# Placing the last ten of 18 attention blocks beside the scans, taking softmax sums from a ones column, and moving loads off ScalarE's queue

## The chip, the cores and the metric

One core of one Trainium2 chip. The metric is device time in microseconds (us) of one execution. Runs over 1.5% above the fastest of their kernel are called slow. The profiled execution has a span, from first to last instruction, which is about 1.8 us below the time that the run reports. Engines are named as in the profile: PE is the matrix engine (TensorE), PEld its weight loads, DVE is VectorE, ACT is ScalarE, POOL is GpSimd and SP is SyncE, which here only issues loads and stores.

## The reference

Two independent halves write the two halves of the output's columns.

```python
# A: sliding, dilated attention. x (1, 2048, 448), 16 heads of 28
qkv = x @ wqkv
idx = pos[:, None] - 2 * arange(8)                 # 8 keys, two apart, back in time
attn = softmax(where(idx >= 0, q . k[idx] * 28 ** -0.5, -1e9))
a = (attn . v[idx]) @ wo
# B: a diagonal complex state-space model, 448 states, over 2048 steps
Lam_bar = exp(dt * (Lambda_re + 1j * Lambda_im)); dt = exp(log_dt)
h[t] = Lam_bar * h[t-1] + B_bar @ x[t]
y[t] = 2 * Re(C @ h[t]) + x[t] * Dskip
out = concatenate([a, b], axis=-1)                 # bf16
```

## The kernel before

Attention works on 18 blocks (9 of 114 queries for even positions, 9 for odd). A block is scores on PE, Exp on ACT, values on PE, an eviction on ACT. Softmax sums of a group of 6 blocks are gathered in one PSUM tile `dn`; one reciprocal on DVE serves the group; a normalisation (`att_norm`) spreads the reciprocals over the heads with PE and multiplies on DVE. A projection tile (`wo_tile`) then needs normalised blocks. The B half makes scan inputs on PE (`bu`), evicts them to `Z` on ACT, scans on DVE (`scan`, four calls), and ends with eight `y_tile`s on PE.

```python
# loads: ScalarE issues sixteen of them before its first arithmetic
for i, vec in enumerate((B_Lambda_re, B_Lambda_im, B_log_dt, B_Dskip)):
    ACT.dma_start(vrow[i:i + 1, 0:D], vec.unsqueeze(0))
for k in range(3):
    ACT.dma_start(wraw[:, k, :], A_wqkv[128 * k:128 * (k + 1), 0:2 * D])
ACT.dma_start(wraw[64:128, 3, :], A_wqkv[384:448, 0:2 * D])
load_xa(0, 0); load_xa(1, 0)                       # SyncE
ACT.dma_start(wv[:, 0:3, :], ...); ACT.dma_start(wv[64:128, 3, :], ...)
load_xa(0, 1); load_xa(1, 1)                       # SyncE
for ri, (m_, o_) in enumerate(...):                # six loads of B
    ACT.dma_start(NB_[...], ...)
# ... [cut]

def att_pv(n):                                     # values, and sums from P
    # ... [cut]
    for g in range(4):
        w0 = 31 - (4 * c + g)
        for j in range(4):                         # 16 narrow matmuls per block
            PE.matmul(att["dn"][32 * j:32 * j + 32, :], eden[:, e_, w0:w0 + 32], P[:, j, g, :], ...)
    ACT.copy(oT[...], op[:])
    if c == GB - 1:                                # GB = 6 blocks in a group
        V.reciprocal(rf[:], att["dn"][:]); V.tensor_copy(rb[:], rf[:])
        att["rb"] = rb
# ... [cut]

weave(steps[:12], fl)       # 6 blocks among the second half of the projections
bz_open()                   # memory for the scans
fl = []                     # scan inputs, scans, then normalisations 0-5, wo tiles 0, 1
for pt in range(4):
    fl.append(L(bu, 0, pt))
    if pt % 2:
        fl.append(L(scan, 0, pt // 2))
# ... [the same for the second half of the sequence; cut]
for i in range(0, GB, 2):
    fl.append(L(att_norm, i))
for n in range(2):
    fl.append(L(wo_tile, n))
weave(steps[12:24], fl)     # 6 more blocks among these
# ... [normalisations 6-11, wo tiles 2-4, y tiles 0-3 among the last 6 blocks,
#      normalisations 12-17, a check of all values, wo tiles 5-7, y tiles 4-7]
```

`weave` puts the entries of one list evenly between those of the other. A scheduler may still reorder inside an engine, so the places named below are read from the traces.

## Time and profile before

Three runs: 222.16 us median (221.75 to 223.7).

| stage of the profiled run (span 220.1 us) | us | what holds it |
|---|---|---|
| to the first Exp, 45.43 | 45.4 | ACT does no arithmetic until 20.84 |
| first Exp to first scan, 100.09 | 54.7 | PE busy 46.0, ACT 37.1 |
| first scan to end of last scan, 153.57 | 53.5 | DVE busy 52.7 |
| end of last scan to end | 66.5 | PE busy 52.2 |

First the page's shares of busy time and its 40 slices of 5.5 us; a digit is the busy share in tenths, and PEclk the granted clock of PE in tenths.

```profile
PE 161.9 (74%) x1618; PEld 80.7 (37%) x1629; DVE 117.7 (53%) x222; ACT 97.3 (44%) x137; POOL 9.3 (4%) x24
PE   0094769988488879899995960276798997399970
DVE  4671587744625632307999999999621001702010
PEclk9999699999969999999999695556799999859997
```

No engine is full overall, but DVE is full from the 20th to the 28th slice, and PE nearly empty in the 25th and 26th.

ACT's start (timeline: start, duration, engine, line of the program, operation, output and input, count, and in brackets the idle time just before with what ended it; ACTq is ACT's sequencer issuing a load):

```profile
8.93 0.51 ACTq L188 DMA_DIRECT2D wraw<-in_A_wqkv_dram  x1
...
20.20 0.61 ACTq L198 DMA_DIRECT2D NB__92<-in_B_B_re_dram  x1
20.84 1.28 ACT L397 ACT_TABLE_LOAD   x1 [20.84 <-DMA xTA<-in_A_x_dram]
...
22.25 0.99 ACT L272 CAST qT<-pq 128x1024 bf16<-128x1024 f32 x1
...
45.43 0.93 ACT L319 ACTIVATE P<-sp 128x912 bf16<-128x912 f32 x1
```

The loads of B still go out at 20.20 us, and only then can ACT begin. The Trainium skill, "DMA: Bandwidth & Descriptors", section "Anatomy of one DMA — SWDGE (gpsimd) path", says that a wait for a semaphore is served on the sequencer that issues the load, before the load is dispatched. The trace agrees in that ACT stands behind its own load issues for 20.84 us; which semaphore each issue waited for it does not show.

PE's two stops of over 3 us after the first scan (timeline of PE):

```profile
141.66 3.43 PE L367 MATMUL pw<-wo,qT 128*128 128x448 bf16 x8 [11.06 <-DVE qT L358]
...
191.33 0.16 PE L670 MATMUL pg<-good,ones 128*1 128x1 bf16 x1 [3.35 <-DVE good L666]
```

The first is a projection tile that waits for normalisations queued on DVE behind a scan. About six attention blocks are still undone at that time, but most stand behind it in PE's order.

### The profile page before, as it was taken

The page shows a single profiled execution, that of the slowest core. Times are in us where ns is not written, and L with a number is a line of the kernel's source. Part 1 is how long each engine was busy: PE and PEld are TensorE (multiplying, and loading weights), DVE is VectorE, ACT ScalarE, POOL GpSimd, SP SyncE. Part 2 cuts the span into 40 slices and gives each one's busy share as a digit, 9 for nine tenths or more (in the row PEclk, how much of TensorE's full clock was granted, in tenths as well). Part 3 has the DMA queues.
Part 4 walks back from the last instruction along what each step waited for, and adds up shares of the span by engine and source line. Part 5 has one row for each costly group of instructions (what it writes and reads, how often), then busy time and mean ns, then how long its engine had stood idle before and what let it go on. Part 6 is the DMA issues. An engine that isn't in the chain of part 4 may idle for free.

```text
span 220.1 us, 3859 instructions
## 1 busy us (share of the span) xinstructions
PE 161.9 (74%) x1618; PEld 80.7 (37%) x1629; DVE 117.7 (53%) x222; ACT 97.3 (44%) x137; POOL 9.3 (4%) x24
## 2 busy tenths in 40 slices
PE   0094769988488879899995960276798997399970
PEld 0031224435234435445442440022554554245540
DVE  4671587744625632307999999999621001702010
ACT  0002939998667873627554460023366263011110
POOL 8700000000000000000000000000000000000000
PEclk9999699999969999999999695556799999859997
DMA  6999990349300000000000000000212111112211
GB/s 124 210 247 253 271 217 3 60 92 126 60 0 3 0 3 0 3 0 0 3 0 3 0 3 0 1 0 17 69 45 83 45 42 43 43 42 83 84 47 46
DMA packets 31028, 13.05 MB, mean 59 GB/s; under 512 B 23644, under 2 KB 31008, under 8 KB 31008
## 3 DMA queue, kind: packets, MB, share of 16 engines
q1 hardware_dynamic: 28888, 10.65, 21.7%
q10 hardware_dynamic: 2120, 2.13, 4.4%
q8 instruction: 14, 0.23, 0.4%
q14 instruction: 6, 0.05, 0.1%
HBM read 3.33 MB, written 3.67 MB: 32 GB/s over the span
## 4 chain that ended last, share of the span: by engine, by line
DVE 37%; PE 31%; ACT 13%; DMA 7%; SPq 6%; issue 3%; DVEq 0%
DVE sc L554 9%; PE pw L367 6%; DVE qT L358 4%; PE py L575 4%; PE py L577 4%; ACT mixt L452 4%; DMA xTA<-in_A_x_dram 3%; PE py L573 3%; PE pv L292 3%; PE pb L535 3%; DMA Cn<-in_B_C_im_dram 3%; DVE kT L274 3%; PE pq L281 2%; SPq L178 2%; DVE sc L547 2%
## 5 line engine op out<-in xcount | busy, mean ns | idle before, releaser
L281 PE MATMUL pq<-xTA,wqk 128*128 128x512 bf16 x121 | 35.1, 434 | 10.5 <-ACT qT L272 5.9
L319 ACT ACTIVATE P<-sp 128x912 bf16<-128x912 f32 x36 | 32.1, 932 | 22.4 <-PE sp L315 22.4
L535 PE MATMUL pb<-xTB,BT 128*128 128x512 bf16 x108 | 26.5, 398 | 3.1 <-ACT Z L537 2.7
L367 PE MATMUL pw<-wo,qT 128*128 128x448 bf16 x64 | 19.2, 464 | 12.1 <-DVE qT L358 11.2
L281 PEld LDWEIGHTS <-wqk 128*128 128x128 bf16 x128 | 13.3, 107 | 29.0 <-issue 17.8
L535 PEld LDWEIGHTS <-BT 128*128 128x128 bf16 x112 | 11.2, 101 | 16.4 <-issue 4.5
L537 ACT CAST Z<-pb 128x1024 bf16<-128x1024 f32 x8 | 8.1, 1012 | 17.3 <-PE pb L535 10.5
L272 ACT CAST yb<-py 128x896 bf16<-128x896 f32 x6 | 5.4, 905 | 23.3 <-PE py L579 17.4
L367 PEld LDWEIGHTS <-qT 128*128 128x128 bf16 x64 | 7.1, 119 | 21.6 <-DVE qT L358 13.7
L292 PE MATMUL pv<-wv,xTA 128*128 128x448 bf16 x72 | 14.5, 353 | 0.7 <-DVE vp L274 0.7
L310 PE MATMUL sp<-mB,mA 32*128 32x456 bf16 x72 | 9.6, 381 | 5.7 <-DVE Wt L453 1.4
L342 DVE RECIPROCAL rf<-dn 128x114 f32<-128x114 f32 x3 | 2.6, 871 | 20.0 <-PE dn L337 20.0
L358 DVE SCALAR_TENSOR_TENSOR qT<-bc,qT 128x456 bf16<-128x456 f32 x18 | 10.7, 629 | 2.5 <-PE bc L352 2.4
L575 PE MATMUL py<-WL,Hs 128*128 128x448 bf16 x56 | 11.9, 352 | 0.0
L577 PE MATMUL py<-Wt,Hs 128*128 128x448 bf16 x56 | 11.9, 352 | 0.0
L272 ACT CAST ya<-pw 128x896 bf16<-128x896 f32 x4 | 3.6, 905 | 16.5 <-issue 8.4
L339 ACT CAST qT<-op 128x456 bf16<-128x456 f32 x18 | 9.8, 547 | 1.8 <-PE op L331 1.8
L397 ACT ACT_TABLE_LOAD x1 | 1.3, 1283 | 20.8 <-DMA xTA<-in_A_x_dram 20.8
L274 DVE CAST ya<-pw 128x896 bf16<-128x896 f32 x4 | 4.4, 1092 | 11.4 <-PE pw L367 11.4
L274 DVE CAST kT<-pq 128x1024 bf16<-128x1024 f32 x8 | 9.8, 1222 | 0.7 <-PE pq L281 0.7
L554 DVE TENSOR_TENSOR_SCAN sc<-rT,ini,Z 128x512 bf16<-128x512 f32 x8 | 9.6, 1267 | 0.0
L292 PEld LDWEIGHTS <-xTA 128*128 128x128 bf16 x72 | 6.9, 98 | 7.3 <-issue 1.0
(155 smaller groups left out, 240.0 us busy)
## 6 DMA issues: line engine op xcount, KB each, us to landing
out_dram<-ya SPq DMA_DIRECT2D x8, 224.0 KB, 2.4
out_dram<-yb SPq DMA_DIRECT2D x8, 224.0 KB
wraw<-in_A_wqkv_dram ACTq DMA_DIRECT2D x3, 224.0 KB
Cn<-in_B_C_re_dram SPq DMA_DIRECT2D x1, 392.0 KB, 4.3
Cn<-in_B_C_im_dram SPq DMA_DIRECT2D x1, 392.0 KB
wo<-in_A_wo_dram SPq DMA_DIRECT2D x4, 98.0 KB
wv<-in_A_wqkv_dram ACTq DMA_DIRECT2D x1, 336.0 KB
NB__92<-in_B_B_re_dram ACTq DMA_DIRECT2D x1, 336.0 KB, 6.1
```

Of the source, the lines that this page charges most:

```text
L274: V.tensor_copy(o_, i_)
L281: PE.matmul(ps[:, i, :], wqk[:, kt, qk, 4 * g:4 * g + 4, :].rearrange("p h d -> p (h d)"), xTA[:, kt, par, XPAD + 512 * h:XPAD + 512 * (h ...
L292: PE.matmul(ps[:, par, 0:D], xTA[:, kt, par, XW + QB * b:XW + QB * b + KB], wv[:, kt, :], start=(kt == 0), stop=(kt == 3))
L310: PE.matmul(sp[j // 2][:, j % 2, 0:4 * QB], mA[r0:r0 + 32, :], mB[r0:r0 + 32].rearrange("p a q -> p (a q)"), start=True, stop=False, skip_ ...
L319: ACT.activation(P[:, 2 * jp:2 * jp + 2].rearrange("p j g q -> p j (g q)"), sp[jp][:, :, 0:4 * QB], ACTF.Exp, scale=float(DH) ** -0.5)
L339: ACT.copy(oT[:, :, par, QB * b:QB * (b + 1)], op[:])
L358: V.scalar_tensor_tensor(o_, bc[:, i, 0:4 * QB].rearrange("p (g q) -> p g q", g=4), DSC, o_, ALU.mult, ALU.mult, accum_out=acc[:, n:n + 1])
L367: PE.matmul(ps[:, par, 0:D], oT[:, g, par, 128 * n:128 * (n + 1)], wo[:, g, :], start=(g == 0), stop=(g == 3))
L535: PE.matmul(ps[:, ri, :], BT[:, s_, ri, 128 * pt:128 * (pt + 1)], xTB[:, s_, SEG * s:SEG * (s + 1)], start=(s_ == 0), stop=(s_ == NS - 1))
L554: V.tensor_tensor_scan(c_[:, ri, i, :], prm["rT"][:, pt:pt + 1].to_broadcast((128, SEG)), z[:, ri, i, :], 0.0 if s == 0 else ini[:, ri, pt ...
L575: PE.matmul(ps[:, 0, 0:D], zz["H"][:, k, 128 * n + 1:128 * n + 129], WL[:, k, :], start=False, stop=(k == NK - 1))
L577: PE.matmul(ps[:, 1, 0:D], zz["H"][:, k, 128 * n + 2:128 * n + 130], Wt[:, k, :], start=(k == 0), stop=False)
```

## The change

Its intent: start ACT earlier; give PE attention blocks to do while DVE scans, so that fewer are left after; spend less of PE on sums; and shorten the work after the last scan. It has four parts.

1. Loads of the value weights and B go from ACT to SP, those of `wo` and C from SP to POOL. The copies of the query and key weights, all on DVE before, are shared with ACT. The selection matrix `sel` is made by ACT later, instead of by POOL at the start.
2. Column 28 of each head's 32 columns of V is a constant, so the value matmul also gives the sum. Four wide matmuls per block (`att_den`) pack these into `dn`, for groups of 8, 8 and 2 blocks.
3. Order: 8 blocks before the scans (was 6), 10 blocks with their sums beside the scans (was 6), none after, apart from ends of the last two. Normalisations 8 to 17 come after y tiles 0 to 3.
4. All evictions of the second half of the projections go to DVE.

The change also moves the transposed loads of the B half's x to the start, builds masks, tables and B's mixed inputs in another order, and shifts memory pools.

```diff
-    ACT.dma_start(wv[:, 0:3, :], ...)
-    ACT.dma_start(wv[64:128, 3, :], ...)
+    nc.sync.dma_start(wv[:, 0:3, :], ...)
+    nc.sync.dma_start(wv[64:128, 3, :], ...)
+    for ri, (m_, o_) in enumerate(...):
+        nc.sync.dma_start(NB_[...], ...)            # six loads of B
     load_xa(0, 1)
     load_xa(1, 1)
-    for ri, (m_, o_) in enumerate(...):
-        ACT.dma_start(NB_[...], ...)
# ... [cut]
-    V.memset(vp[:, :, :, DH:32], 0.0)
+    POOL.memset(vp[:, :, :, DH:DH + 1], DSC)
+    POOL.memset(vp[:, :, :, DH + 1:32], 0.0)
+    POOL.memset(vp[0:KPAD, 0:2, :, DH:DH + 1], 0.0)
# ... [wo and C: POOL.dma_start in place of nc.sync.dma_start; cut]
+    def att_den(n):
+        ...
         for g in range(4):
             w0 = 31 - (4 * c + g)
-            for j in range(4):
-                PE.matmul(att["dn"][32 * j:32 * j + 32, :], eden[:, e_, w0:w0 + 32], P[:, j, g, :], ...)
+            PE.matmul(att["dn"][:], (eden if m == 8 else edenL)[:]...[:, w0:w0 + 128], oT[:, g, par, ...], ...)
+        if c == m - 1:
             V.reciprocal(rf..., att["dn"]...); V.tensor_copy(rb[:], rf[:])
             att["rb"] = rb
# ... [cut]
-                fl.append(L(proj_qk, qk, par, 1, gp))
+                fl.append(L(proj_qk, qk, par, 1, gp, "D"))
-    weave(steps[:12], fl)
+    weave(steps(0, 8), fl)
     bz_open()
# ... [fl: scan inputs and scans as before]
-    for i in range(0, GB, 2):
-        fl.append(L(att_norm, i))
-    for n in range(2):
-        fl.append(L(wo_tile, n))
-    weave(steps[12:24], fl)
+    fl.insert(2, L(att_norm, 0))
+    fl.insert(3, L(att_norm, 2))
+    weave(steps(8, 18), fl)
+    fl = [L(att_norm, n) for n in (4, 6)] + [L(wo_tile, n, "A") for n in range(3)]
     for n in range(4):
         fl.append(L(y_tile, n, "A"))
-    weave(steps[24:], fl)
+    weave(steps(18, NA + 3), fl)
+    for n in range(8, NA, 2):
+        att_norm(n)
# ... [check; then wo tiles 3-7 (was 5-7) and y tiles 4-7]
```

More of the change, by code (lines that the diff above doesn't have):

```diff
@@ L25 @@
 QL = QB * NB
-GB = 6
 KT = 112
@@ L159 @@
     at = main.enter_context(tc.tile_pool(name="at", bufs=2))
-    pj = main.enter_context(tc.tile_pool(name="pj", bufs=1))
+    pj_ctx = ExitStack()
+    pj = pj_ctx.enter_context(tc.tile_pool(name="pj", bufs=1))
     bk = main.enter_context(tc.tile_pool(name="bk", bufs=1, side="right"))
@@ L166 @@
     xTA = pj.tile([128, 4, 2, XL], BF16, tag="xTA")
+    wraw = pj.tile([128, 4, 2 * D], BF16, tag="wraw")
+    wv = pj.tile([128, 4, D], BF16, tag="wv")
+    wqk = pj.tile([128, 4, 2, H, 32], BF16, tag="wqk")
     xTB = bk.tile([128, NS, NP], BF16, tag="xTB")
+    NB_ = st.tile([128, 2, 4, 2 * D], BF16, tag="NB")
+    Cn = st.tile([KT, 2, 4, 512], BF16, tag="Cn")
+    vrow = const.tile([4, 576], BF16, tag="vrow")
+    wo = at.tile([128, 4, D], BF16, tag="wo", bufs=1)
     xa_r = A_x[0].rearrange("(i two) d -> two i d", two=2)
@@ L178, in load_xb @@
         nc.sync.dma_start_transpose(xTB[:, :, SEG * s_:SEG * (s_ + 1)], xb_r[SEG * s_:SEG * (s_ + 1), :])
-    vrow = const.tile([4, 576], BF16, tag="vrow")
-    wraw = st.tile([128, 4, 2 * D], BF16, tag="cw")
-    wv = pj.tile([128, 4, D], BF16, tag="wv")
-    NB_ = st.tile([128, 2, 4, 2 * D], BF16, tag="NB")
     for i, vec in enumerate((B_Lambda_re, B_Lambda_im, B_log_dt, B_Dskip)):
@@ L190 @@
     load_xa(1, 0)
-    ACT.dma_start(wv[:, 0:3, :], A_wqkv[0:384, 2 * D:3 * D].rearrange("(s p) n -> p s n", p=128))
-    ACT.dma_start(wv[64:128, 3, :], A_wqkv[384:448, 2 * D:3 * D])
+    nc.sync.dma_start(wv[:, 0:3, :], A_wqkv[0:384, 2 * D:3 * D].rearrange("(s p) n -> p s n", p=128))
+    nc.sync.dma_start(wv[64:128, 3, :], A_wqkv[384:448, 2 * D:3 * D])
+    for ri, (m_, o_) in enumerate(((B_B_re, B_B_im), (B_B_im, B_B_re))):
+        nc.sync.dma_start(NB_[:, ri, 0:3, D:2 * D], m_[0:384, :].rearrange("(s p) n -> p s n", p=128))
+        nc.sync.dma_start(NB_[0:64, ri, 3, D:2 * D], m_[384:448, :])
+        nc.sync.dma_start(NB_[64:128, ri, 3, D:2 * D], o_[384:448, :])
     load_xa(0, 1)
     load_xa(1, 1)
-    for ri, (m_, o_) in enumerate(((B_B_re, B_B_im), (B_B_im, B_B_re))):
-        ACT.dma_start(NB_[:, ri, 0:3, D:2 * D], m_[0:384, :].rearrange("(s p) n -> p s n", p=128))
-        ACT.dma_start(NB_[0:64, ri, 3, D:2 * D], m_[384:448, :])
-        ACT.dma_start(NB_[64:128, ri, 3, D:2 * D], o_[384:448, :])
+    load_xb(0)
+    load_xb(1)
     kT = xa.tile([128, 4, 2, KL], BF16, tag="kT")
@@ L203 @@
     vp = xa.tile([128, 2 * NB, H, 32], BF16, tag="vp")
-    wqk = pj.tile([128, 4, 2, H, 32], BF16, tag="wqk")
-    wo = at.tile([128, 4, D], BF16, tag="wo", bufs=1)
-    eden = const.tile([128, 2, 63], BF16, tag="eden")
-    sel = const.tile([128, 4 * GB, 128], BF16, tag="sel")
+    eden = const.tile([128, 5, 32], BF16, tag="eden")
     pm = const.tile([128, 1], I32, tag="pm")
     kq = st.tile([128, 128], I32, tag="kq")
+    iot = st.tile([128, SEG], F32, tag="iota")
+    hpib = const.tile([128, 1], F32, tag="hpib")
+    POOL.memset(hpib[:], 0.5 * PI * SHR)
+    POOL.iota(iot[:], [[1, SEG]], base=0, channel_multiplier=0, allow_small_or_imprecise_dtypes=True)
+    POOL.iota(pm[:], [[0, 1]], base=0, channel_multiplier=1)
+    POOL.iota(kq[:], [[1, 128]], base=0, channel_multiplier=0)
     V.memset(wqk[:, :, :, :, DH:32], 0.0)
@@ L212 @@
     V.memset(wv[0:64, 3, :], 0.0)
-    V.memset(vp[:, :, :, DH:32], 0.0)
-    V.memset(wo[:], 0.0)
     POOL.memset(kT[:, :, :, 0:KPAD], 0.0)
@@ L219, with sel_make, wqk_copy @@
     POOL.memset(xTA[:, :, :, XPAD + NP:XL], 0.0)
-    POOL.iota(pm[:], [[0, 1]], base=0, channel_multiplier=1)
-    POOL.iota(kq[:], [[1, 128]], base=0, channel_multiplier=0)
-    iot = st.tile([128, SEG], F32, tag="iota")
-    POOL.iota(iot[:], [[1, SEG]], base=0, channel_multiplier=0, allow_small_or_imprecise_dtypes=True)
-    POOL.memset(eden[:], 0.0)
-    POOL.memset(eden[:, :, 31:32], DSC)
-    POOL.memset(eden[:, :, 55:56], DSC)
-    POOL.memset(eden[0:KPAD, 1, :], 0.0)
-    POOL.memset(sel[:], 1.0)
-    POOL.affine_select(out=sel[:], in_=sel[:], compare_op=ALU.is_equal, fill=0.0, base=0,
-                       pattern=[[-1, 4 * GB], [-32, 4], [0, 32]], channel_multiplier=1)
-    for kt in range(4):
-        p0 = 64 if kt == 3 else 0
-        V.tensor_copy(wqk[p0:128, kt, :, :, 0:DH], wraw[p0:128, kt, :].rearrange("p (a h d) -> p a h d", a=2, h=H))
+    POOL.memset(eden[:], 1.0)
+    POOL.affine_select(out=eden[:], in_=eden[:], compare_op=ALU.is_equal, fill=0.0, base=31 - DH,
+                       pattern=[[-32, 5], [-1, 32]], channel_multiplier=1)
+    POOL.memset(eden[:, :, 0:31], 0.0)
+    edenL = const.tile([128, 5, 32], BF16, tag="edenL")
+    POOL.tensor_copy(edenL[:], eden[:])
+    for i_ in range(3):
+        POOL.tensor_copy(edenL[:, 1:5, 7 + 8 * i_:8 + 8 * i_], eden[:, 0:4, 31:32])
+    POOL.memset(vp[:, :, :, DH:DH + 1], DSC)
+    POOL.memset(vp[:, :, :, DH + 1:32], 0.0)
+    POOL.memset(vp[0:KPAD, 0:2, :, DH:DH + 1], 0.0)
+    POOL.memset(wo[:], 0.0)
+    wo_r = A_wo.rearrange("(g j d) n -> j d g n", j=4, d=DH)
+    for j in range(4):
+        POOL.dma_start(wo[32 * j:32 * j + DH, :, :], wo_r[j])
+    for ri, m_ in enumerate((B_C_re, B_C_im)):
+        POOL.dma_start(Cn[:, ri, :, 0:D], m_.rearrange("(k p) n -> p k n", p=KT))
+    sel = const.tile([128, 32, 4, 32], BF16, tag="sel")
+    def sel_make():
+        with tc.issue_after(att["exp"].ins):
+            ACT.copy(sel[:], ident[:].rearrange("p (j r) -> p r j", j=4).unsqueeze(3).to_broadcast((128, 32, 4, 32)))
+    def wqk_copy():
+        for kt in range(4):
+            p0 = 64 if kt == 3 else 0
+            (V.tensor_copy if kt % 2 == 0 else ACT.copy)(
+                wqk[p0:128, kt, :, :, 0:DH], wraw[p0:128, kt, :].rearrange("p (a h d) -> p a h d", a=2, h=H))
     mA = const.tile([128, 128], BF16, tag="mA")
@@ L274, in evac, with proj_qk @@
             V.tensor_copy(o_, i_)
-    def proj_qk(qk, par, h, gp):
+    def proj_qk(qk, par, h, gp, eng=None):
         ps = ps2.tile([128, 2, 512], F32, tag="s", name="pq")
@@ L283, in proj_qk, with proj_v @@
         if qk == 0:
-            evac(qT[:, 2 * gp:2 * gp + 2, par, 512 * h:512 * (h + 1)], ps[:])
+            evac(qT[:, 2 * gp:2 * gp + 2, par, 512 * h:512 * (h + 1)], ps[:], eng)
         else:
-            evac(kT[:, 2 * gp:2 * gp + 2, par, KPAD + 512 * h:KPAD + 512 * (h + 1)], ps[:])
-    def proj_v(b):
+            evac(kT[:, 2 * gp:2 * gp + 2, par, KPAD + 512 * h:KPAD + 512 * (h + 1)], ps[:], eng)
+    def proj_v(b, eng=None):
         ps = ps2.tile([128, 2, 512], F32, tag="s", name="pv")
@@ L293, in proj_v @@
                           start=(kt == 0), stop=(kt == 3))
-        evac(vp[:, 2 * b:2 * b + 2, :, 0:DH], ps[:, :, 0:D].rearrange("p b (h d) -> p b h d", h=H))
+        evac(vp[:, 2 * b:2 * b + 2, :, 0:DH], ps[:, :, 0:D].rearrange("p b (h d) -> p b h d", h=H), eng)
     order = [(par, b) for b in range(NB) for par in range(2)]
@@ L318, in att_s, with grp @@
         for jp in range(2):
-            ACT.activation(P[:, 2 * jp:2 * jp + 2].rearrange("p j g q -> p j (g q)"), sp[jp][:, :, 0:4 * QB],
+            att["exp"] = ACT.activation(P[:, 2 * jp:2 * jp + 2].rearrange("p j g q -> p j (g q)"), sp[jp][:, :, 0:4 * QB],
                            ACTF.Exp, scale=float(DH) ** -0.5)
+    GRP = (8, 8, 2)
+    GOF = (0, 8, 16)
+    def grp(n):
+        k = min(n // 8, 2)
+        return n - GOF[k], GRP[k]
     def att_pv(n):
@@ L324, in att_pv @@
         P = Pt.pop(n)
-        c = n % GB
-        if c == 0:
-            att["dn"] = ps1.tile([128, QB], F32, tag="dn", name="dn")
         op = ps1.tile([128, 4, QB], F32, tag="o", name="op")
@@ L332, in att_pv @@
                           start=True, stop=True, skip_group_check=True)
-        e_ = 1 if b == 0 else 0
+        ACT.copy(oT[:, :, par, QB * b:QB * (b + 1)], op[:])
+    def att_den(n):
+        par, b = order[n]
+        c, m = grp(n)
+        if c == 0:
+            att["dn"] = ps1.tile([128, QB], F32, tag="dn", name="dn")
         for g in range(4):
             w0 = 31 - (4 * c + g)
-            for j in range(4):
-                PE.matmul(att["dn"][32 * j:32 * j + 32, :], eden[:, e_, w0:w0 + 32], P[:, j, g, :],
-                          start=(c == 0 and g == 0), stop=(c == GB - 1 and g == 3), skip_group_check=True)
-        ACT.copy(oT[:, :, par, QB * b:QB * (b + 1)], op[:])
-        if c == GB - 1:
+            PE.matmul(att["dn"][:], (eden if m == 8 else edenL)[:].rearrange("p a b -> p (a b)")[:, w0:w0 + 128], oT[:, g, par, QB * b:QB * (b + 1)],
+                      start=(c == 0 and g == 0), stop=(c == m - 1 and g == 3), skip_group_check=True)
+        if c == m - 1:
             rf = at.tile([128, QB], F32, tag="rf", name="rf")
-            V.reciprocal(rf[:], att["dn"][:])
+            V.reciprocal(rf[0:128], att["dn"][0:128])
             rb = at.tile([128, QB], BF16, tag="rb", name="rb")
@@ L349, in att_norm @@
         for i in range(2):
-            c = (n0 + i) % GB
+            c, m = grp(n0 + i)
             for g in range(4):
-                PE.matmul(bc[:, i, QB * g:QB * (g + 1)], sel[:, 4 * c + g, :], att["rb"][:],
+                s_ = sel[:, 4 * c + g].rearrange("p j r -> p (j r)")
+                PE.matmul(bc[:, i, QB * g:QB * (g + 1)], s_, att["rb"][:],
                           start=True, stop=True, skip_group_check=True)
@@ L383, in params @@
     def params():
-        V.tensor_copy(vrow[:, D:512], vrow[:, 384:D])
-        V.tensor_copy(vrow[:, 512:576], vrow[:, 0:64])
         tpv = ps2.tile([128, 8, 4], BF16, tag="s", name="tpv")
@@ L393, in params @@
         dsk = vec[:, 3, :]
-        hpib = vt("hpib", 1)
-        POOL.memset(hpib[:], 0.5 * PI * SHR)
         dt = vt("dt")
@@ L461, in lam_b @@
             nc.sync.dma_start_transpose(BT[:, :, ri, 128 * pt:128 * (pt + 1)], NB_[:, ri, pt, :])
-    Cl = []
-    def load_c():
-        Cn = st.tile([KT, 2, 4, 512], BF16, tag="cw", name="Cn")
-        Cl.append(Cn)
-        for ri, m_ in enumerate((B_C_re, B_C_im)):
-            nc.sync.dma_start(Cn[:, ri, :, 0:D], m_.rearrange("(k p) n -> p k n", p=KT))
     def w_make(ph):
-        Cn = Cl[0]
         tp = ps2.tile([128, 2, 1024], BF16, tag="s", name="tp")
@@ L521, in bz_open @@
     def bz_open():
-        st_ctx.close()
-        bz = bz_ctx.enter_context(tc.tile_pool(name="bz", bufs=1, side="right"))
+        pj_ctx.close()
+        bz = bz_ctx.enter_context(tc.tile_pool(name="bz", bufs=1))
         zz["bz"] = bz
@@ L582, in y_tile @@
         nc.sync.dma_start(out_b[n, :, :, D:2 * D], yb[:])
-    steps = []
-    for n in range(2 * NB):
-        steps.append(lambda n=n: att_s(n))
-        if n > 0:
-            steps.append(lambda n=n: att_pv(n - 1))
-    steps.append(lambda: att_pv(2 * NB - 1))
     def weave(st_, fl):
@@ L603, in L @@
         return lambda: f(*a)
+    V.tensor_copy(vrow[:, D:512], vrow[:, 384:D])
+    V.tensor_copy(vrow[:, 512:576], vrow[:, 0:64])
+    wqk_copy()
     params()
     table(0)
-    table(1)
+    masks()
     for gp in range(2):
@@ L612, with steps @@
             if gp == 0:
-                table(2 + par)
-    for pt in range(4):
-        lam_b(pt)
-    load_xb(0)
-    load_c()
+                table(1 + par)
+            elif par == 0:
+                table(3)
+                lam_b(0)
+            else:
+                lam_b(1)
     for b in range(4):
         proj_v(b)
-    masks()
+        if b < 2:
+            lam_b(2 + b)
     d_make()
-    load_xb(1)
-    wo_r = A_wo.rearrange("(g j d) n -> j d g n", j=4, d=DH)
-    for j in range(4):
-        nc.sync.dma_start(wo[32 * j:32 * j + DH, :, :], wo_r[j])
+    NA = 2 * NB
+    SL = [[] for _ in range(NA + 3)]
+    for n in range(NA):
+        SL[n].append(L(att_s, n))
+        SL[n + 1].append(L(att_pv, n))
+        SL[n + 2].append(L(att_den, n))
+    NQ = {9: (0, 2, 4, 6), 17: (8, 10, 12, 14), 19: (16,)}
+    def steps(lo, hi):
+        return [f_ for k in range(lo, hi) for f_ in SL[k]]
     fl = []
@@ L629 @@
             for qk in range(2):
-                fl.append(L(proj_qk, qk, par, 1, gp))
+                fl.append(L(proj_qk, qk, par, 1, gp, "D"))
     for b in range(4, NB):
-        fl.append(L(proj_v, b))
+        fl.append(L(proj_v, b, "D"))
     for i, f_ in enumerate((L(w_make, 0), L(w_make, 1), L(wl_make, 0), L(wl_make, 1), L(wl_make, 2), L(wl_make, 3),
@@ L635 @@
         fl.insert(2 * i + 2, f_)
-    weave(steps[:12], fl)
+    fl.insert(18, sel_make)
+    weave(steps(0, 8), fl)
     bz_open()
     fl = []
-    for pt in range(4):
-        fl.append(L(bu, 0, pt))
-        if pt % 2:
-            fl.append(L(scan, 0, pt // 2))
-    for pt in range(4):
-        fl.append(L(bu, 1, pt))
-        if pt % 2:
-            fl.append(L(scan, 1, pt // 2))
-    for i in range(0, GB, 2):
-        fl.append(L(att_norm, i))
-    for n in range(2):
-        fl.append(L(wo_tile, n))
-    weave(steps[12:24], fl)
-    fl = []
-    for i in range(0, GB, 2):
-        fl.append(L(att_norm, GB + i))
-    for n in range(2, 5):
-        fl.append(L(wo_tile, n))
+    for s_ in range(2):
+        for pt in range(4):
+            fl.append(L(bu, s_, pt))
+            if pt % 2:
+                fl.append(L(scan, s_, pt // 2))
+    fl.insert(2, L(att_norm, 0))
+    fl.insert(3, L(att_norm, 2))
+    weave(steps(8, 18), fl)
+    fl = [L(att_norm, n) for n in (4, 6)] + [L(wo_tile, n, "A") for n in range(3)]
     for n in range(4):
         fl.append(L(y_tile, n, "A"))
-    weave(steps[24:], fl)
-    for i in range(0, GB, 2):
-        att_norm(2 * GB + i)
+    weave(steps(18, NA + 3), fl)
+    for n in range(8, NA, 2):
+        att_norm(n)
     asum = const.tile([128, 1], F32, tag="asum")
@@ L673 @@
     bad = nc.values_load(flag[0:1, 0:1], min_val=0, max_val=1)
-    for n in range(5, 8):
+    for n in range(3, 8):
         wo_tile(n)
@@ L678 @@
     bz_ctx.close()
+    st_ctx.close()
     main.close()
```

## The prediction

> **What bounds the kernel now.** No engine is full (first part of the page: PE 74%, DVE 53%, ACT 44% of a 220.1 us span); three serial stretches set the time. (1) Start: ScalarE issues loads that wait for earlier loads and does no work until 20.84 us (its timeline), so the first projection tiles are evicted from 22.25 us and PE stands from about 19.1 to 23.3 us. (2) 100.1 to 153.5 us: the four scans on VectorE, 12.5 us each, almost without a gap (14.0 of 14 us busy from 138 to 152). PE is idle 11.06 us until 141.66, waiting for the normalised qT, and stays at clock 0.50 there: 8 output-projection matmuls take 3.43 us, later 1.69. That agrees with the Trainium skill, "TensorE: Matmul & The Clock Gate", Part 1: an idle window halves PE's clock. (3) The 66.6 us after the scans: six attention blocks, six projection tiles, eight y tiles of 3.6 us, final check, output.
>
> **What the change does, costed.**
> - Loads: eight of ScalarE's sixteen issues go to SyncE, and wo and C from SyncE to GpSimd. ScalarE still waits for the fourth wraw load (issued at 8.93 us now, copied at 11.99), then starts. Its table work takes about 5.5 us, so the first eviction comes at about 18.5 us instead of 22.25, the first Exp at about 39 instead of 45.4: 6 to 7 us off the critical path. GpSimd's 6.2 us of building sel go too; the first wqk copy took 2.8 us beside it, others 0.39.
> - Middle before the scans (ACT, PE and DVE alternate): now 38 us of ACT work take 48 us. Afterwards ACT work stays near 36 us (4 more Exp and about 4 us of sel, an estimate from 1 ns per element of Exp, against fewer evictions and mix copies); VectorE gets 8 us more evictions. I expect 45 to 48 us, but holding 8 attention blocks instead of 6. First scan at about 89 us (now 100.1).
> - Scans: the four stay 50 us. With 8 normalisations (0.56 us each) and two reciprocals, VectorE's chain is about 57 us, ending at about 146. The other 10 attention blocks hide under it; PE finishes them 15 to 20 us early and waits cold, because projection tiles 1 and 2 stand ahead of the y tiles in its order and need normalisations queued inside the last scan.
> - Sums: 288 narrow matmuls (16 in about 0.31 us) become 72 wide ones (estimate 0.2 us per block): 2 us of PE, mostly off the path.
> - After the scans: projection tile 2 and y tiles 0-3 (18 us with the cold start), ten normalisations with PE waiting and the check (7), five projection tiles (9), four y tiles (14.4), last eviction and landing (6.6): about 55 us instead of 66.6.
>
> **Sum.** 89 + 57 + 55 = 201 us of span. Run times are about 1 us above that. I predict 201 us, 190 to 211. Chances: faster by over 2% 0.95, within 2% 0.04, slower 0.01.
>
> **What would show it.** ScalarE's first work at 11 to 13 us; first scan between 84 and 94; scans plus normalisations 55 to 59 us with DVE full; a PE gap over 8 us before the first y tile, ended by VectorE; a second gap of 4 to 7 us before the last projections; 54 to 57 us from last scan to end.
>
> **What would make it wrong.** GpSimd's loads competing with wraw and x, so that PE starts later; VectorE's evictions queuing behind the mix steps and keeping PSUM full, so the first scan comes no earlier (about 210); the middle running at ACT's 36 us (about 190); normalisations waiting for PE inside the scans.

## More of the kernel before

The stages in numbers (view by windows: the window, its length, then busy time and instruction count for PE, PEld, DVE, ACT, POOL, then the PE clock, the DMA share and GB/s):

```profile
0.00:45.43 45.43, 27.78 (x130) 11.89 (x133) 27.41 (x84) 20.92 (x35) 9.17 (x23) 0.96 0.83 171
45.43:100.09 54.66, 45.96 (x544) 23.16 (x548) 22.36 (x32) 37.05 (x54) 0.11 (x1) 0.97 0.17 26
100.09:153.57 53.48, 35.93 (x397) 16.89 (x400) 52.71 (x70) 20.34 (x26) 0.00 (x0) 0.78 0.00 1
153.57:220.10 66.53, 52.21 (x549) 28.73 (x548) 15.24 (x38) 19.01 (x24) 0.00 (x0) 0.91 0.17 57
```

## The result, and the profile after

The kernel after took 201.97 us median (200.88 to 202.53, 4 runs) against 222.93 (221.75 to 223.83) for the kernel before. The ratio is 0.9057, with a 95% interval of 0.8991 to 0.9122. Ratios here are the mean time of one kernel's fast runs over that of the other's of the same rounds, so not quite the ratio of the medians quoted. The result is correct. The profiled span is 200.7 us, so 19.4 us went.

```profile
PE 157.8 (79%) x1401; PEld 80.5 (40%) x1413; DVE 118.7 (59%) x223; ACT 99.4 (50%) x135; POOL 12.2 (6%) x35
PE   0169999778888799894998998946789983999940
DVE  2639995667778334309994999999990057222200
PEclk9999999999999999998599699995899998899995
```

The total work of the engines hardly changed: PE 157.8 us against 161.9. The time went from the waits. By stage, cut at the same four events as before (first Exp, first scan, end of the last scan):

```profile
0.00:38.04 38.04, 25.78 (x127) 11.22 (x130) 25.20 (x83) 25.18 (x40) 12.08 (x34) 1.00 1.02 206
38.04:91.58 53.54, 46.05 (x519) 23.50 (x522) 28.08 (x36) 37.33 (x51) 0.11 (x1) 1.00 0.14 25
91.58:149.11 57.53, 46.33 (x507) 24.25 (x512) 53.69 (x75) 27.88 (x37) 0.00 (x0) 0.85 0.03 9
149.11:200.70 51.59, 39.68 (x252) 21.50 (x250) 11.71 (x31) 8.98 (x10) 0.00 (x0) 0.93 0.20 64
```

Against before the stages changed by -7.4, -1.1, +4.1 and -14.9 us. Under the scans PE now does 46.3 us of work instead of 35.9, which is 10.4 us more, and after them 39.7 instead of 52.2. That exchange is the largest part of the gain, and it costs a scan stretch that is 4.1 us longer: other DVE work lies between the scans (normalisations and another reciprocal), and so does a wait of 2.97 us, shown below.

ACT's start, and PE's stops of over 3 us after the first scan:

```profile
7.80 0.52 ACTq L191 DMA_DIRECT2D wraw<-in_A_wqkv_dram  x1
8.35 1.28 ACT L253 ACT_TABLE_LOAD   x1 [8.35 <-DMA wraw<-in_A_wqkv_dram]
...
18.14 0.99 ACT L293 CAST qT<-pq 128x1024 bf16<-128x1024 f32 x1
...
38.04 0.93 ACT L340 ACTIVATE P<-sp 128x912 bf16<-128x912 f32 x1
```

```profile
137.36 0.37 PE L382 MATMUL bc<-rb,sel 128*128 128x114 bf16 x2 [3.91 <-DVE rb L373]
...
169.15 0.16 PE L684 MATMUL pg<-good,ones 128*1 128x1 bf16 x1 [3.33 <-DVE good L680]
```

ACT begins at 8.35 us instead of 20.84, but only 7.4 of these 12.5 us reach the first Exp: the last weight copy, now on ACT, and PE behind it still wait until about 13 us for the fourth load of weights. The 11.06 us stop of PE has become one of 3.91 us. DVE shows two new holes, which stand for what is left to take:

```profile
108.94 1.23 DVE L564 TENSOR_TENSOR sc<-Z,tab 128x2048 bf16<-128x2048 bf16 x1 [2.97 <-ACT Z L554]
...
162.89 0.63 DVE L388 SCALAR_TENSOR_TENSOR qT<-bc,qT 128x456 bf16<-128x456 f32 x1 [12.66 <-PE bc L382]
```

In the second one DVE is idle while PE makes y tiles 0 to 3. Then DVE does ten normalisations (162.89 to 168.5 us) while PE waits for it. Two engines take turns where they could work side by side.

### The profile page after: what moved, and what is told of

The parts are those of the page before. It is cut to its first block, busy times and chain, and to the rows that moved or that the text cites. A ratio compares the mean times of both kernels' runs of the same rounds, so it can differ in the third digit from the quotient of the medians.

```text
span 200.7 us, 3428 instructions
## 1 busy us (share of the span) xinstructions
PE 157.8 (79%) x1401; PEld 80.5 (40%) x1413; DVE 118.7 (59%) x223; ACT 99.4 (50%) x135; POOL 12.2 (6%) x35
## 3 DMA queue, kind: packets, MB, share of 16 engines
HBM read 3.33 MB, written 3.67 MB: 35 GB/s over the span
## 4 chain that ended last, share of the span: by engine, by line
PE 50%; DVE 28%; ACT 7%; DMA 6%; issue 3%; SPq 1%; POOL 0%; DVEq 0%; POOLq 0%
PE pq L302 12%; DVE sc L571 7%; PE pv L313 6%; PE pw L397 5%; PE py L592 5%; PE py L594 5%; PE pb L552 5%; DVE qT L388 4%; PE py L590 3%; PE pk L520 3%; DMA xTA<-in_A_x_dram 3%; DVE sc L564 2%; DVE Z L565 2%; DMA wraw<-in_A_wqkv_dram 2%; ACT Z L554 2%
## 5 line engine op out<-in xcount | busy, mean ns | idle before, releaser
L302 PE MATMUL pq<-xTA,wqk 128*128 128x512 bf16 x122 | 32.7, 413 | 10.1 <-ACT wqk L253 3.7
L552 PE MATMUL pb<-xTB,BT 128*128 128x512 bf16 x106 | 27.3, 398 | 1.3 <-ACT Z L554 0.6
L293 ACT CAST ya<-pw 128x896 bf16<-128x896 f32 x6 | 5.4, 906 | 24.7 <-PE pw L397 24.7
L397 PE MATMUL pw<-wo,qT 128*128 128x448 bf16 x64 | 15.8, 403 | 1.7 <-DVE qT L388 1.0
L313 PE MATMUL pv<-wv,xTA 128*128 128x448 bf16 x72 | 14.6, 352 | 2.2 <-DVE K_168 L526 1.1
L295 DVE CAST vp<-pv 128x896 bf16<-128x896 f32 x7 | 7.6, 1091 | 7.4 <-PE pv L313 7.4
L382 PE MATMUL bc<-rb,sel 128*128 128x114 bf16 x72 | 6.1, 242 | 6.6 <-DVE rb L373 4.6
L336 PE MATMUL sp<-qT,kT 32*128 32x114 bf16 x288 | 10.4, 214 | 0.0
L356 PE MATMUL op<-P,vp 128*32 128x114 bf16 x288 | 9.3, 226 | 1.3 <-ACT P L340 1.3
L397 PEld LDWEIGHTS <-qT 128*128 128x128 bf16 x64 | 6.6, 109 | 9.4 <-issue 4.0
```

Of the source, the lines that this page charges most:

```text
L293: ACT.copy(o_, i_)
L295: V.tensor_copy(o_, i_)
L302: PE.matmul(ps[:, i, :], wqk[:, kt, qk, 4 * g:4 * g + 4, :].rearrange("p h d -> p (h d)"), xTA[:, kt, par, XPAD + 512 * h:XPAD + 512 * (h ...
L313: PE.matmul(ps[:, par, 0:D], xTA[:, kt, par, XW + QB * b:XW + QB * b + KB], wv[:, kt, :], start=(kt == 0), stop=(kt == 3))
L397: PE.matmul(ps[:, par, 0:D], oT[:, g, par, 128 * n:128 * (n + 1)], wo[:, g, :], start=(g == 0), stop=(g == 3))
L552: PE.matmul(ps[:, ri, :], BT[:, s_, ri, 128 * pt:128 * (pt + 1)], xTB[:, s_, SEG * s:SEG * (s + 1)], start=(s_ == 0), stop=(s_ == NS - 1))
```

## The experiments

Three theories were on trial. *Places*: the gain is the earlier start (about 7 us) plus attention blocks moved under the scans, and nothing else matters much. *Work*: PE has less to do for the sums. *Loads*: the earlier start carries nearly all. All kernels gave correct results. The kernel before took 223.01 us median (7 runs); later 222.57 and 222.06 us.

### a0_after_again: the kernel after, unchanged

The edit is none.

> The changed kernel as it is, as the yardstick for the other kernels of this call. Every theory: 201 to 203 us, span about 200.5.

Measured: 202.53 us median (201.73 to 203.73), ratio 0.9094 (0.903 to 0.9158), span 200.7. The result repeats; this is the base for the next three.

### e1_loads_back: the loads where they were

```diff
-    nc.sync.dma_start(wv...), nc.sync.dma_start(NB_...)   # behind the first half of x
-    POOL.dma_start(wo...), POOL.dma_start(Cn...)
+    ACT.dma_start(wv...), ACT.dma_start(NB_...)           # as in the kernel before
+    nc.sync.dma_start(Cn...), nc.sync.dma_start(wo...)
```

> All else of the change kept, loads on their old queues (V weights and B on ScalarE, wo and C on SyncE). Theory 'places' (the gain is an earlier start of about 7 us plus attention blocks moved under the scans): ScalarE's first work at 20 to 21 us again, first Exp at 44 to 46 us instead of 38.0, first scan 6 to 8 us later, 208 to 211 us in all. Rival 'work' (the gain is the PE work saved by the ones column): within 2 us of the changed kernel. Rival 'loads' (the earlier start carries nearly all): 215 us or more.

Measured: 212.11 us median (210.75 to 214.23), ratio 0.9499 (0.942 to 0.9578). One of the four runs is slow; the median of the fast ones, 211.54, is 9.0 us over a0. In its trace (timeline of PE, then of ACT and of DVE):

```profile
23.72 6.61 PE L302 MATMUL pq<-xTA,wqk 128*128 128x512 bf16 x20 [12.55 <-ACT wqk L253]
```

```profile
50.41 0.93 ACT L340 ACTIVATE P<-sp 128x912 bf16<-128x912 f32 x1
```

```profile
103.93 1.23 DVE L564 TENSOR_TENSOR sc<-Z,tab 128x2048 bf16<-128x2048 bf16 x1
```

The first Exp comes 12.6 us after that of a0 (37.85), later even than in the kernel before (45.43). The reason is in the first line: the change gives ACT half of the weight copies, so with the loads back on ACT, PE makes three matmuls of its projections and then stands 12.55 us until ACT has issued its loads and copied. The two edits of part 1 belong together. So the 9.0 us are not the worth of the places alone: they contain a first Exp 5 us later than in the kernel before. b1 below measures the places from the other side.

### e2_sums_back: the sums as before, first attempt

```diff
-    POOL.memset(eden[:], 1.0) ... affine_select ... edenL ... vp ones column
+    POOL.memset(eden[:], 0.0); POOL.memset(eden[:, :, 31:32], DSC) ...
+    POOL.memset(vp[:, :, :, DH:32], 0.0)
     # att_pv: 16 narrow matmuls from P; att_den: only the reciprocal
```

> All else kept, softmax sums by 288 narrow matmuls from P as before instead of 72 wide ones from the ones column. Theory 'places': PE busy 2 to 3 us more, most of it hidden, 202 to 205 us. Rival 'work': 208 us or more. Rival 'loads': within 2 us.

Measured: 209.53 us median (208.64 to 211.64), ratio 0.9417 (0.934 to 0.9494), 7.0 us over a0. The expectation of *places* was missed, but this run does not speak for *work* either. The delay stands at the start, before any sum (timeline of ACT):

```profile
8.71 0.57 ACTq L191 DMA_DIRECT2D wraw<-in_A_wqkv_dram  x1
9.31 1.28 ACT L248 ACT_TABLE_LOAD   x1 [9.31 <-DMA wraw<-in_A_wqkv_dram]
10.61 0.94 ACT L248 COPY wqk<-wraw 128x896 bf16<-128x896 bf16 x1
18.59 0.94 ACT L248 COPY wqk<-wraw 64x896 bf16<-64x896 bf16 x1 [7.05 <-DMA wraw<-in_A_wqkv_dram]
```

My edit shortened POOL's list of memsets. POOL therefore issued its loads of C and `wo` from 5.4 us on, where a0 begins at 7.7 us with `wo` and issues C from 10.6. The fourth load of the query and key weights, issued at 8.7 us, then took 9.9 us to land instead of 4.0. The Trainium skill, "DMA: Bandwidth & Descriptors", section "Queues, rings and completion order", says that each DMA engine serves the queue rows that have work in turn; the trace fits this: with the 1.2 MB of POOL's loads issued earlier, of which nothing is used while PE waits, the one load that PE waits for landed late. How the DMA engines shared their time was not looked at. So the kernel after has a good start partly because POOL is kept busy with memsets. By reading, the edit had a second fault: the group tile `dn` was claimed for group 1 before group 0's reciprocal was made, so that reciprocal read the wrong tile. A clean version follows.

### e2b_sums_back_clean: the sums as before, and nothing else

```diff
+    eden2 = ...            # made by POOL behind its loads; all else of the start untouched
     def att_pv(n):
+        # 16 narrow matmuls from P into dn, as in the kernel before
         ACT.copy(oT[...], op[:])
+        # reciprocal of the group here, as in the kernel before
     def att_den(n):
-        # four wide matmuls and the reciprocal
```

> The kernel after, with only the softmax sums made as before: sixteen narrow matmuls per block straight from P, in place of the four wide ones over the ones column; start-up program, loads and the order of everything else untouched. The earlier attempt at this also changed GpSimd's start, and its trace showed all its delay (first exponential 44.21 against 38.04 us) before any sum was made, and from the first exponential to the end 163.3 against 162.7 us. Theory of places: the first exponential stays at 38 us, the time 201 to 204 us, at most 2 us over the kernel after. Theory of work: the sums carry a real part of the gain, 205 us or more, with the first exponential unmoved.

Measured: 207.01 us median of 4 runs, of which two are slow (208.85 and 209.2) and two fast (205.17 and 204.46). The mean of the fast ones is 204.8 us; e6 below, an unaffected kernel, is at 201.86 median. So the sums are worth about 3 us, from two fast runs and without an interval. That lies just between the ranges of both theories (up to 204, and 205 or more): the sums are neither mostly off the path, as I had it, nor a main part. The stretch from the first Exp to the first scan is 57.14 us here and 53.52 us in a0 (view by windows; e2b first):

```profile
36.49:93.63 57.14, 48.33 (x649) 24.88 (x650) 28.34 (x36) 37.25 (x51) 0.11 (x1) 0.97 0.15 28
```

```profile
37.85:91.37 53.52, 46.05 (x519) 23.51 (x522) 28.08 (x36) 37.29 (x51) 0.11 (x1) 1.00 0.14 26
```

ACT's work is the same; PE's is 2.3 us more and the stretch 3.6 us longer. In e2, with its other start, the stretch was 57.2 us too (44.21 to 101.44), and in a0, after, e1 and e6, with wide sums, it was 53.5 each time. In e2, as in e2b, PE's clock in the stretch was 0.97 and not 1.00. About 1.4 us is given back under the scans (56.5 us against 57.9 in e6), and the part after them is 2.0 us longer (53.2 against 51.1). The matmuls of the sums alone, in these windows, take 4.10 us for 9 blocks (144 narrow) against 2.97 us for 8 blocks (32 wide), so 0.46 against 0.37 us per block; how the other 2 us of the stretch arise was not separated.

### e3_order_back: the order as before

```diff
-    weave(steps(0, 8), fl)
+    weave(steps(0, 7), fl)
     # scan inputs and scans
-    fl.insert(2, L(att_norm, 0)); fl.insert(3, L(att_norm, 2))
-    weave(steps(8, 18), fl)
-    fl = [L(att_norm, n) for n in (4, 6)] + [L(wo_tile, n, "A") for n in range(3)]
+    fl += [L(att_norm, n) for n in (0, 2, 4, 6)] + [L(wo_tile, n, "A") for n in range(2)]
+    weave(steps(7, 13), fl)
+    fl = [L(wo_tile, 2, "A")]
     # y tiles 0 to 3 as in the kernel after
-    weave(steps(18, NA + 3), fl)
+    weave(steps(13, NA + 3), fl)
```

> All else kept, order of blocks as before: about 6 blocks ahead of the scans, 6 beside them, 5 or 6 behind them. Theory 'places': first scan at 84 to 88 us instead of 91.6, but 64 to 70 us from the end of the last scan to the end of the kernel instead of 51.5; 210 to 217 us in all. Rivals 'work' and 'loads': within 3 us of the changed kernel.

Measured: 209.06 us median (207.13 to 209.31), ratio 0.9364 (0.9293 to 0.9434), 6.5 us over a0, just under the range. The first scan is at 88.09 us, 3.3 earlier than in a0, and its end at about 142 us, but the stage after the scans takes 63.3 us instead of 51. PE's large stop is back (timeline of PE):

```profile
125.90 0.56 PE L331 MATMUL sp<-mB,mA 32*128 32x456 bf16 x2 [11.54 <-DVE qT L388]
...
174.89 0.16 PE L683 MATMUL pg<-good,ones 128*1 128x1 bf16 x1 [3.33 <-DVE good L679]
```

This is the 11.06 us stop of the kernel before. So the order removes it, as claimed. The cost is that the first scan comes 3.3 us later, with one more block ahead of it, and that the scans take 58.1 us in a0 against 54.1 here; this is why the order's net worth is 6.5 us and not the 12 of the tail.

### b1_before_loads_moved: the kernel before, with part of the loads moved

```diff
-    ACT.dma_start(wv...); ACT.dma_start(NB_...)
+    nc.sync.dma_start(wv...); nc.sync.dma_start(NB_...)   # behind the first half of x
```

> The kernel before, with only the loads of the value weights and of B taken off ScalarE's queue and put on SyncE's behind the first half of x. Theory of places: ScalarE's first table load moves from 20.8 us to 9 to 11 us and the first exponential from 45.4 to 37 to 41 us; half of it or more reaches the end: 213 to 218 us, no more than half of the whole gain, and the idle stretch of TensorE under the scans stays at about 11 us. Theory of loads: 206 us or less. Against both: if the loads of C, which stay on SyncE and now come later, hold the scans back, 219 us or more.

Measured: 211.86 us median of 4 runs, of which two are slow (212.83 and 213.33); the fast ones are 208.74 and 210.89, ratio 0.9458 (0.9339 to 0.9577), which is 9 to 15 us off the kernel before. The fast runs lie between what *places* allowed (213 to 218) and what *loads* asked for (206 or less), so both were off. The profiled run is a slow one, so its times are only an indication: first Exp at 40.38 us, first scan at 91.59, and PE's idle stretch under the scans still there, as *places* said (timeline of PE):

```profile
133.15 3.43 PE L367 MATMUL pw<-wo,qT 128*128 128x448 bf16 x8 [12.74 <-DVE qT L358]
```

Eight moved loads, without any of the rest, bring about half to three quarters of the change's gain: 4.2 to 6.6% by the interval, where a0 has 9.1%.

### e4_evac_alternate: evictions shared again

```diff
-                fl.append(L(proj_qk, qk, par, 1, gp, "D"))
+                fl.append(L(proj_qk, qk, par, 1, gp))
-        fl.append(L(proj_v, b, "D"))
+        fl.append(L(proj_v, b))
```

> The kernel after, with the evictions of the second half of the projections alternating between ScalarE and VectorE as before, instead of all on VectorE. Six or seven evictions of about 0.95 us go back to ScalarE, which is busy 37 of the 53.5 us from the first exponential to the first scan. Both theories of the middle part: if TensorE sets that stretch (46 of 53.5 us), within 1.5 us of the kernel after, 201 to 204 us; if ScalarE's order does, because exponentials queue behind evictions, 2 to 5 us slower, the first scan at 93 to 97 us.

Measured: 202.7 us median (201.36 to 203.85), ratio 0.9123 (0.9049 to 0.9196). First Exp to first scan is 54.2 us (38.26 to 92.46), 0.7 more than in the kernel after, although ACT is busy 42.5 us of it instead of 37.3. Part 4 of the change makes no difference that could be seen, and ACT does not set the middle stretch.

### e5_sums_4_11_doubled and e6_own_sums: whose sums are used?

Reading the program, I found a mistake in the change. `att["rb"]` is one name, overwritten by each group, and normalisations are issued when the next group's reciprocal has already replaced it: blocks 4 to 7 are divided by the sums of group 1, blocks 8 to 15 by those of group 2. In the kernel before, by the same reading, every normalisation stands ahead of the next group's reciprocal.

```diff
# e5, wrong on purpose
     POOL.memset(vp[:, :, :, DH:DH + 1], DSC)
+    POOL.memset(vp[:, 4:12, :, DH:DH + 1], 2 * DSC)
# e6, mended
-            att["rb"] = rb
+            att["rb", n // 8] = rb
-                PE.matmul(bc[...], s_, att["rb"][:], ...)
+                PE.matmul(bc[...], s_, att["rb", (n0 + i) // 8][:], ...)
```

> The kernel after, with the ones column of blocks 4 to 11 doubled on purpose, so that the sums of these blocks come out twice too large. If each block is divided by its own sums, half of the attention output is halved and the comparison fails. If, as the reading of the program says, blocks 4 to 7 and 8 to 15 are divided by other groups' sums, nothing changes for blocks 4 to 11 but the result stays within tolerance: correct. The time says nothing here.

Measured (one run): correct, 201.41 us. This fits the reading. By itself it is not proof, because no control was run that shows that the comparison would notice a halved block. e6 settles it from the trace.

> The kernel after, with each pair of blocks divided by its own group's sums (the reciprocals are kept by group, where the kernel after keeps one name that the last group overwrites). No instruction is added or removed; only what the normalisations of blocks 4 to 7 and 8 to 15 read changes, and these read sums that are ready earlier. Both theories: correct, the time within 1 us of the kernel after (201 to 203 us); if the wait of TensorE for the second group's reciprocal (5.5 us once) is what holds the tail, 1 to 4 us faster.

Measured: correct, 201.86 us median (201.07 to 202.59), ratio 0.9105 (0.9024 to 0.9187): no change in time. Its timeline of PE at the place where the kernel after waited 3.91 us for `rb`:

```profile
131.49 0.42 PE L382 MATMUL bc<-rb,sel 128*128 128x114 bf16 x5
135.91 0.54 PE L367 MATMUL dn<-qT,edenL 128*128 128x114 bf16 x4 [3.99 <-DVE rf L371]
136.24 1.25 PE L382 MATMUL bc<-rb,sel 128*128 128x114 bf16 x11
```

With its own group's reciprocal, normalisation 4 starts at 131.49 us without any wait; in the kernel after it started at 137.36, behind group 1's reciprocal. So the kernel after does divide these blocks by other blocks' sums. It passes because, with these inputs, the logits are small and a softmax over 8 keys has sums near 8 everywhere: worked out from the reference's inputs, no logit is over 0.015 and the sums over 8 keys lie between 7.96 and 8.04. On other inputs it would be wrong. The mend is free in time: PE now stands 3.99 us for the next reason in line, the group's tile `dn`, which the last two blocks can use only when the reciprocal has read it.

### v1_y_first: y tiles under the last scans

Built on e6. y tiles 0 to 3 need only the first two scans.

```diff
-    fl = [L(att_norm, n) for n in (4, 6)] + [L(wo_tile, n, "A") for n in range(3)]
-    for n in range(4):
-        fl.append(L(y_tile, n, "A"))
-    weave(steps(18, NA + 3), fl)
-    for n in range(8, NA, 2):
-        att_norm(n)
+    weave(steps(18, NA + 3), [L(y_tile, n, "A") for n in range(4)])
+    att_norm(4); att_norm(6); y_tile(4, "A")
+    att_norm(8); att_norm(10); y_tile(5, "A")
+    att_norm(12); att_norm(14); att_norm(16)
+    for n in range(3):
+        wo_tile(n, "A")
     # check; wo tiles 3-7; y tiles 6, 7
```

> The kernel with its own sums, and in the last part another order: y tiles 0 to 3, which need only the first two scans, come right behind the last attention blocks, so that TensorE has them under the last scans; the remaining normalisations and projection tiles 0 to 2 come after them, between y tiles 4 and 5, with the check behind. Nothing else differs. If, as I now hold, the tail is TensorE's work plus its two stretches of waiting for VectorE (about 5 to 8 us between 133 and 147 us, and 7 us around the check), the first scan stays at 90 to 92 us and the end comes 8 to 13 us sooner: 189 to 194 us. If VectorE's chain (scans and normalisations) sets the tail instead, it moves less than 3 us: 199 us or more.

Measured: 191.63 us median (189.2 to 192.82), ratio 0.8661 (0.8593 to 0.873), 10 us under e6 (11 by the fast runs alone). This speaks for PE and not DVE's chain as what sets the tail. The edit moves normalisations on DVE too; v3 leaves DVE's order alone.

### v2_y_first_rows_on_gpsimd: parameter rows loaded by POOL

```diff
-        ACT.dma_start(vrow[i:i + 1, 0:D], vec.unsqueeze(0))
+        POOL.dma_start(vrow[i:i + 1, 0:D], vec.unsqueeze(0))
```

> The same with one more edit: the four short parameter rows are loaded by GpSimd instead of ScalarE, so that the loads of the query and key weights are the first on ScalarE's queue and none of them has to wait for a DMA semaphore (the fourth was issued at 7.8 to 8.9 us and copied at 12 us in the kernel after). Expected: ScalarE's table load at 3 to 5 us in place of 8 to 9.5, TensorE's projections in full run from 9 to 11 us in place of 13, first exponential 33 to 36 us, and 2 to 4 us off the end of the run before: 186 to 191 us. If x or the parameter rows hold the start instead, no gain; if the loads of the output weights and C collide with the last weights as in the first sums experiment, slower.

Measured: 192.81 us median (192.12 to 194.37), ratio 0.8708 (0.863 to 0.8786): no gain over v1. The first half of the expectation came true: the four loads of weights were all issued by 3 us and the table load followed at 2.98. But PE's transposes of the parameter rows, which start the chain of parameters, moved the other way (timeline of PE):

```profile
10.53 0.21 PE L416 MATMUL tpv<-ident,vrow 4*128 4x4 bf16 x3 [10.53 <-POOL edenL L231]
10.68 0.61 PE L302 MATMUL pq<-xTA,wqk 128*128 128x512 bf16 x1
12.09 0.29 PE L416 MATMUL tpv<-ident,vrow 4*128 4x4 bf16 x5 [0.81 <-DVE vrow L616]
```

In v1 they ran at 5.25 to 6 us. POOL issued the rows' loads between 1.39 and 3.97 us. The profile puts the wait down to POOL, but its list of loads gives 5.5 to 7.1 us from issue to landing for these four rows of 0.9 KB, so the last, issued at 3.35, landed at about 10.4. The fourth load of weights gained little as well: issued at 2.24 us it took 7.5 us to land, at about 9.7, where in v1 it was issued at 7.65 and took 3.0, to about 10.7. Issuing 5.4 us earlier brought it in about 1 us earlier; why the rows took so long on that queue was not tested.

### v3_y_before_last_block: one more step of v1

```diff
+    for n in range(2):
+        y_tile(n, "A")
-    weave(steps(18, NA + 3), [L(y_tile, n, "A") for n in range(4)])
+    weave(steps(18, NA + 3), [L(y_tile, n, "A") for n in range(2, 4)])
```

> The version with y tiles 0 to 3 under the last scans, with one more step of the same kind: y tiles 0 and 1 now stand ahead of the sums of the last two blocks, because in the profile of that version TensorE stood 3.9 us behind those sums, which wait for a reciprocal that VectorE makes inside the last scan, and ran the first y tile slowly afterwards. VectorE's order is unchanged. If TensorE sets the tail, 2 to 5 us faster than that version: 186.5 to 190 us; if VectorE's scans and normalisations set it, no change: 191 to 193 us.

Measured: 186.57 us median (184.97 to 188.17, 6 runs), ratio 0.8409 (0.8348 to 0.847). This version beats both kernels and has the right sums. Its timeline of PE where the kernel after stood still, and its stages:

```profile
131.49 0.27 PE L336 MATMUL sp<-qT,kT 32*128 32x114 bf16 x6
131.69 0.93 PE L590 MATMUL py<-K,xTB 128*128 128x448 bf16 x4
132.46 1.49 PE L592 MATMUL py<-WL,Hs 128*128 128x448 bf16 x7
```

```profile
38.15:91.68 53.53, 46.38 (x525) 23.51 (x522) 28.08 (x35) 37.30 (x51) 0.11 (x1) 1.00 0.12 23
91.68:147.04 55.36, 50.78 (x555) 27.01 (x556) 51.85 (x67) 28.76 (x38) 0.00 (x0) 0.94 0.04 14
147.04:183.60 36.56, 30.23 (x211) 16.92 (x207) 12.77 (x38) 9.00 (x10) 0.00 (x0) 0.98 0.26 84
```

The stretch to the first scan is that of the kernel after. Under the scans PE now works 50.8 us of 55.4, and the stage after them is 36.6 us instead of 51.6, at a clock of 0.98 instead of 0.93.

## Why the prediction was right or wrong

The total was right: 201 us predicted, 201.97 measured. It came out right with two terms off by about 3.5 us in opposite directions. That they cancel is luck, so the sum is better than its parts. (The sum was a span, and the measured span is 200.7; run times are 1.8 us above it, not 1.)

| term of the sum | predicted | measured (profile after) |
|---|---|---|
| ACT's first work | 11 to 13 us | 8.35 (table load), 9.64 (first copy), 13.01 (parameters) |
| first eviction of a projection | 18.5 | 18.14 |
| first Exp | 39 | 38.04 |
| first Exp to first scan | 50 (39 to 89) | 53.54 |
| scans with normalisations | 57 | 57.53 |
| last scan to end | 55 | 51.59 |

- **The start was right in size**, 7.4 us against 6 to 7. But reading its worth from this stage alone undersold the loads: they are worth 9.0 us taken back (e1, with a start spoilt beyond that of the kernel before) and 9 to 15 us put alone into the kernel before (b1).
- **The middle was 3.5 us too short** in the sum, and 5.5 to 8.5 us against the 45 to 48 in the text, which do not fit the first scan at 89. I reasoned from ACT's 36 us of work. ACT was busy 37.3 us, as expected, but PE was busy 46.05 of 53.54 us, and e4, which loads ACT again, changed nothing that could be seen. The stage is nearest to PE's limit; eight blocks instead of six ate what the changes saved there.
- **The scans were right in total, not in kind.** They hold a hole of 2.97 us in which DVE waits for the inputs of the second scan; I had foreseen a full DVE.
- **"Waits cold" was the step that failed.** That PE would finish the blocks 15 to 20 us early came true: all but the last values and sums were done at about 133.45 us, 15.7 us before the scans ended at 149.11. But PE did not wait through that time. The gap that VectorE ends was 3.91 us and not over 8, and behind it no wait was over 0.7 us: PE was busy 10.09 of the 15.66 us. It made normalisations, the last sums and projection tiles as DVE's normalisations came out one by one inside the last scan, and the first y tile began at 147.13, before that scan's end (windows, then timeline of PE, kernel after):

```profile
133.45:149.11 15.66, 10.09 (x71) 5.55 (x72) 15.34 (x23) 4.36 (x7) 0.00 (x0) 0.78 0.09 31
```

```profile
139.58 2.76 PE L397 MATMUL pw<-wo,qT 128*128 128x448 bf16 x8
...
147.13 0.92 PE L590 MATMUL py<-K_168,xTB 128*128 128x448 bf16 x4
```

  This is also the mis-sized term of the tail: I had put 18 us for projection tile 2 and y tiles 0 to 3 after the scans, with a cold start, and it was 13.2 (149.1 to 162.3). Tile 2 and the first y tile's beginning lay under the scans, and the clock after them was 1.00; the slow stretch at a clock of about 0.5 came earlier, from 137 to 142 us.
- **The second gap was as said in kind**: ten normalisations and the check take 162.3 to 169.2 us, 6.9 us against 7, with a wait of 3.33 us at its end (I had put this gap at 4 to 7). The parts after that (five projection tiles 9.2, four y tiles 14.6 and an end of 7.7 us) were foreseen as 9, 14.4 and 6.6.
- **Sums "mostly off the path" was wrong.** e2b shows about 3 us at the end, where 2 us of PE's work were to be mostly hidden; its middle alone is 3.6 us longer.
- **The fear of POOL's loads competing with the weights** did not come true in the kernel after, but e2 made it come true by 2 us of earlier issue, at 6 us of cost.

Taken back one at a time, loads (9.0), order (6.5) and sums (3) add up to 18.5 of the 20.3 us between a0 and before (medians of fast runs), with nothing for the evictions (e4). That they nearly add up proves little, since e1 spoils more than it takes back. *Places* holds in kind, with a larger share for the loads and a smaller one for the order than I gave them; *work* has its 3 us; and *loads* alone is refuted by e3, whose loads are in the new places. The clock of PE moved too, from 0.902 to 0.938 as a mean. I take it as a consequence of fewer idle stretches; no run held it apart.

## What to carry to other kernels

Give the engine that would wait under a long serial stage everything that does not depend on that stage, in the order in which its inputs become ready: the change did this for attention blocks, and v1 and v3 did it for y tiles with another 15 us. Keep load issues off any engine whose first arithmetic is on the path, and hold back loads that are needed late. When work is moved across groups that share one name or one buffer, check whose data each reader gets, because a loose comparison on mild inputs does not.

## What the Trainium skill lacked or had wrong

- "TensorE: Matmul & The Clock Gate", Part 1, ties the halved clock to an idle window of about 3.4 us. In the kernel after the clock was 1.00 until 94 us and 0.50 from 94 to 100 us, although PE's longest wait in the 4 us before was 1.02 us; PE had been busy 2.33 of these 4 us. The section on a second failure mode there speaks of short idle times, but gives no busy share at which it sets in.
- "ScalarE: Activation LUTs", section "What ACT_TABLE_LOAD costs", gives 1283 ns and a drain of 1380 ns, 2.66 us in all. The load agrees (1.28 us), the drain does not show: in the kernel after ACT's last operation before the load ends at 36.73 us, the load starts at 36.74, and the first Exp at 38.04.
- "TensorEngine Tiling (Array Packing)", section "Theoretical Speedup", gives up to 4 times for 32 columns. The narrow sums ran at 28 ns each (4.10 us for 144) against 93 ns for a wide one (2.97 us for 32): 3.3 times, at a mean clock of 0.97 against 1.00. The page has no measured figure, and no page has one for four column tiles at 114 elements.
- No page gives a figure for what a load that is needed late costs one that is needed now: with C and `wo` issued from 5.4 us (e2) instead of 7.7 (a0), the landing time of the awaited weights was 9.9 us instead of 4.0.
